# Gate and up projections by a seven-product block form on pairs of segments, in a fused attention and bilinear GLU kernel

## The chip, the cores and the metric

The kernel runs on one NeuronCore of a Trainium2 chip. A core has a matrix engine (TensorE, PE in the profile, with its weight loads as PEld), a vector engine (VectorE, DVE), a scalar engine (ScalarE, ACT), a general engine (GpSimd, POOL) and an engine that here only issues DMAs (SyncE, SP). Each engine takes its instructions in the order written in its own queue, and engines wait for one another through semaphores. The metric is the device time in microseconds (us).

## The reference, cut to what matters

There are 2048 tokens of width 512. An adaptive layer norm, an attention with a compressive memory over four segments of 512 tokens, and an output projection come first. Then a second layer norm and a bilinear gated unit with inner width F = 1376:

```python
x = x + ga * _A_ref(h, ...)                       # attention with output projection
h = _layernorm(x, axis=-1) * (1 + cb) + sb
g = jnp.einsum("bsd,df->bsf", h, w_gate)
u = jnp.einsum("bsd,df->bsf", h, w_up)
x = x + gb * jnp.einsum("bsf,fd->bsd", g * u, w_down)
```

Only the part from the second layer norm on is changed, with what is prepared for it at the end of the attention.

## The kernel before, in words

All matrix products of this part run in a fast 32-bit format (`float32r`), and to keep the precision each operand is split into a high part (a rounded copy) and a low part (the rest). One product is then three matmuls: high by high, low by high, high by low.

The attention part is written as one hand-ordered stream for PE (the helper `pe`, whose instructions all appear under L85 and L88). A loop over slots issues the attention's steps, and two generators, `fill_a` and `fill_b`, fill the gaps with projections. At the end, `fill_b` runs the output projection of segments 1 and 2 (`wo_mm`, `wo_row`, `wo_add`), the second layer norm of segment 0 (`lnC`), and the weights of the first two tiles of the inner width (`prep(0)`, `prep(1)`, on POOL). After the loop come the output projection of segment 3, in two steps: `wo_row` over the first three head groups, then the transpose and the rows of the last group. Each finished row of x is added by DVE and stored to DRAM (`x1d`) by SP.

Then the gated unit follows, segment by segment (called the last stage below). The inner width is cut into 11 tiles, ten of 128 and one of 96. `gate_up(i)` makes two PSUM banks of 12 matmuls each (four blocks of the 512-wide contraction by three splits, L1122); ACT copies the gate bank to SBUF (L1126), DVE multiplies it with the up bank (L1127), ACT rounds the product to its high part (L1130), DVE subtracts to get the low part (L1131). The down projection of tile i (L1143) comes after `gate_up(i + 1)` on PE and accumulates over all 11 tiles in four PSUM banks per segment; at the end of a segment DVE adds the four banks to x (L1156) and SP stores them (L1157). In segment 0 the weights of each next tile are loaded, split by DVE, ACT and POOL (L429 to L438) and kept for the later segments. The layer norm of the next segment is done inside the current one (at i = 3 and i = 6).

The program's order on each engine is made by a layer that places the instructions by its own costs; within one engine the order is then fixed.

Of the kernel before, what the change touches and what calls it, by code (L numbers as in the profile page):

```python
# [8 lines left out]
F32 = mybir.dt.float32  # L9
# [8 lines left out]
P = 128  # L18
S, D, H, DH, NSEG, L, F = 2048, 512, 32, 16, 4, 512, 1376
KT = D // P  # L20
NG = 4
# [36 lines left out]
def tile_kernel(ctx, tc, x, wq, wk_, wv, wo, beta, w_gate, w_up, w_down, c, w_mod, out):  # L58
# [34 lines left out]
    wpool = ctx.enter_context(tc.tile_pool(name="wp", bufs=1))  # L93
# [298 lines left out]
    wt = {}  # L392

    def prep(i, pool, rpool, tag, nb):

        f0, n = ft[i]
        r, raws = {}, {}
        for w, nm in ((w_gate, "g"), (w_up, "u")):
            raws[nm] = raw = rpool.tile([P, KT, P], F32, tag=tag, name=f"cr{nm}{i}", bufs=nb)
            pin(nc.sync.dma_start(raw[:, :, 0:n], w.rearrange("(k p) f -> p k f", p=P)[:, :, f0:f0 + n]))  # L400
        rawd = rpool.tile([P, D], F32, tag=tag, name=f"crd{i}", bufs=nb)
        pin(nc.sync.dma_start(rawd[0:n], w_down[f0:f0 + n, :]))
        yield 0.0
        if i < 2:
            gp = nc.gpsimd
            for nm in "gu":
                hi = pool.tile([P, KT, P], F32R, name=f"{nm}H{i}", bufs=1)
                r[nm] = (hi, pool.tile([P, KT, P], F32R, name=f"{nm}L{i}", bufs=1))
                pin(gp.tensor_copy(hi, raws[nm]))
                yield 0.0  # L410
            for nm in "gu":
                pin(gp.tensor_sub(r[nm][1], raws[nm], r[nm][0].bitcast(F32)))
                yield 0.0
            hi = pool.tile([P, D], F32R, name=f"dH{i}", bufs=1)
            lo = pool.tile([P, D], F32R, name=f"dL{i}", bufs=1)
            pin(gp.tensor_mul(rawd, rawd, gbb))
            yield 0.0
            pin(gp.tensor_copy(hi, rawd))
            yield 0.0
            pin(gp.tensor_sub(lo, rawd, hi.bitcast(F32)))  # L420
            r["d"] = (hi, lo)
            wt[i] = r
            yield 0.0
            return
        for nm in "gu":
            raw = raws[nm]
            hi = pool.tile([P, KT, P], F32R, name=f"{nm}H{i}", bufs=1)
            lo = pool.tile([P, KT, P], F32R, name=f"{nm}L{i}", bufs=1)
            pin(vec.tensor_copy(hi[:, :, 0:n], raw[:, :, 0:n]))  # L429
            nc.gpsimd.tensor_sub(lo[:, :, 0:n], raw[:, :, 0:n], hi[:, :, 0:n].bitcast(F32))  # L430
            r[nm] = (hi, lo)
            yield 0.0
        hi = pool.tile([P, D], F32R, name=f"dH{i}", bufs=1)
        lo = pool.tile([P, D], F32R, name=f"dL{i}", bufs=1)
        pin(vec.tensor_mul(rawd[0:n], rawd[0:n], gbb[0:n]))
        yield 0.0
        act.activation(hi[0:n], rawd[0:n], AF.Copy)
        nc.gpsimd.tensor_sub(lo[0:n], rawd[0:n], hi[0:n].bitcast(F32))  # L438
        r["d"] = (hi, lo)
        wt[i] = r  # L440
        yield 0.0
# [62 lines left out]
    def lnC(s, pool, hpool, xpool, tag, nb):  # L504
        xt = []
        for t in range(4):
            a = xpool.tile([P, D], F32, tag=tag, name=f"x1_{s}_{t}", bufs=nb)
            nc.sync.dma_start(a, x1d[s][t])
            xt.append(a)
        yield 0.1  # L510
        return (yield from ln(pool, hpool, xt, s, cb_c, sb_c, "c", ("h{}", 1, 1), s > 0))
# [429 lines left out]
    def fill_b():  # L941
# [7 lines left out]
        lg = lnC(0, pb, bc, pb, "x1", 4)  # L949
        pr = prep(0, bc, pb, "cr", 3)  # L950
# [135 lines left out]
    for t in range(4):  # L1086
        run(wo_row(ps3[t], t, us3, range(NG - 1)))
# [16 lines left out]
    for s in range(NSEG):  # L1104
# [30 lines left out]
        for i in range(NF):  # L1135
            if i + 1 < NF:
                gate_up(i + 1)
# [48 lines left out]
```

## Time and profile before

| | |
|---|---|
| median of 3 runs | 898.58 us (898.47 to 899.52) |
| profiled execution, its span from first to last instruction | 898.4 us; the page gives no other time of its own for it |
| PE busy | 870.9 us, 97% of the span |
| DVE, ACT, POOL busy | 523.4, 406.1, 321.2 us |
| last stage: first L1122 matmul to the start of the last L1143 matmul | 522.04 us to 893.50 us |
| mean granted TensorE clock | 0.993 |

A row of a timeline gives the start and the length of an instruction in us, the engine, the source line, the operation and its tiles, a count where rows are merged, and in brackets how long the engine had been idle and for whom it waited. A group row gives count, busy time in us and the mean of one instruction in ns, then the idle time ahead of the group. PE's matmuls are pipelined: the length of one in the profile is longer than the distance from one to the next, and it is the distance that counts. A row of stretches gives, for a stretch of time, each engine's busy time with its count, the granted clock, the busy share of the DMA engines and the rate in GB/s.

### The profile page before, as it was taken

How to read it: one execution, taken by the hardware profiler on the slowest of the kernel's cores; microseconds unless marked ns; L12 is line 12 of the kernel's file. 1: busy time of each engine (PE TensorE's matmuls, PEld its weight loads, DVE VectorE, ACT ScalarE, POOL GpSimd, SP SyncE). 2: the span in 40 equal slices, each digit the busy share in tenths (PEclk: the TensorE clock that was granted, in tenths of full speed). 3: DMA queues.
4: the chain of work that ended last, by engine and by line, in shares of the span. 5: the costliest groups of instructions: out<-in, count | busy, mean ns of one | idle time of the engine just before them, and what ended most of it. 6: DMA issues, size and time to landing. Idle time of an engine off the chain costs nothing.

```text
span 898.4 us, 14218 instructions
## 1 busy us (share of the span) xinstructions
PE 870.9 (97%) x5084; PEld 620.5 (69%) x5084; DVE 523.4 (58%) x1579; ACT 406.1 (45%) x601; POOL 321.2 (36%) x470
## 2 busy tenths in 40 slices
PE   8989999989999999999999999999999999999997
PEld 5755656556665556666666678887888788878886
DVE  7698777888788877778887244552133213321112
ACT  3747757687676865777454512231112111211111
POOL 4445536466455763756337516630000000000000
PEclk8999999999999999999999999999999999999999
DMA  7654434454545555365584344321001100110011
GB/s 219 163 159 130 122 109 124 152 154 130 146 111 156 141 154 129 107 202 166 187 243 140 109 144 126 106 73 71 24 1 47 72 24 1 47 45 3 1 47 47
DMA packets 74951, 97.23 MB, mean 108 GB/s; under 512 B 10528, under 2 KB 47392, under 8 KB 74880
## 3 DMA queue, kind: packets, MB, share of 16 engines
q1 hardware_dynamic: 74736, 96.31, 36.3%
q8 instruction: 40, 0.66, 0.3%
q14 instruction: 31, 0.25, 0.1%
q10 hardware_dynamic: 144, 0.02, 0.0%
HBM read 67.98 MB, written 28.05 MB: 107 GB/s over the span
## 4 chain that ended last, share of the span: by engine, by line
PE 81%; DVE 10%; ACT 5%; issue 1%; DMA 1%; POOL 1%; SPq 0%; DVEq 0%; POOLq 0%
PE gps L1122 14%; PE acc L1143 14%; PE ups L1122 14%; PE tb L85 8%; PE q L85 6%; PE k L85 6%; DVE q L39 5%; PE wops L85 5%; PE vps L85 4%; PE kps L85 4%; PE qps L85 2%; ACT pt L331 2%; PE up L85 1%; PE mz L85 1%; PE tr L88 1%
## 5 line engine op out<-in xcount | busy, mean ns | idle before, releaser
L39 DVE CUSTOM_DVE_ANT_0 q<-q,cmask 128x384 f32<-128x384 f32 (+3 forms) x512 | 246.6, 508 | 49.3 <-PE q L85 39.2
L331 ACT ACTIVATE pt<-k 128x1024 f32<-128x1024 f32 x160 | 163.8, 1024 | 64.4 <-PE k L85 63.3
L337 POOL TENSOR_SCALAR_AFFINE_SELECT pt<-pt 128x256 f32<-128x256 f32 (+1 forms) x224 | 96.7, 446 | 166.0 <-ACT pt L331 163.6
L1127 DVE TENSOR_TENSOR gs<-gs,ups 128x512 f32<-128x512 f32 (+1 forms) x44 | 30.2, 687 | 194.9 <-PE ups L1122 194.9
L85 PE MATMUL q<-kst,qst 96*128 96x384 bf16 (+3 forms) x512 | 101.6, 299 | 11.0 <-DVE nm L39 9.7
L85 PE MATMUL k<-qst,kst 98*128 98x384 bf16 (+3 forms) x512 | 97.1, 302 | 5.0 <-ACT pt L331 4.9
L1126 ACT ACTIVATE gs<-gps 128x512 f32<-128x512 f32 (+1 forms) x44 | 26.2, 597 | 146.3 <-PE gps L1122 146.3
L1130 ACT ACTIVATE mH<-gs 128x512 fp32r<-128x512 f32 (+1 forms) x44 | 27.8, 632 | 130.4 <-DVE gs L1127 128.1
L85 PE MATMUL tb<-pt,v 128*32 128x512 f32 (+3 forms) x1024 | 75.5, 436 | 0.0
L39 DVE DVE_READ_ACCUMULATOR2_ANT nm<- 128x1 f32 x512 | 72.2, 141 | 0.0
L85 PEld LDWEIGHTS <-kst 98*128 98x128 bf16 x512 | 37.7, 98 | 49.5 <-issue 43.2
L1122 PE MATMUL gps<-chH,gL 128*128 128x512 f32 (+1 forms) x176 | 69.3, 394 | 0.0
L1122 PE MATMUL gps<-chH,gH 128*128 128x512 f32 (+1 forms) x176 | 69.3, 394 | 0.0
L1143 PE MATMUL acc<-dH,mL 128*128 128x512 f32 (+1 forms) x176 | 69.3, 394 | 0.0
L1122 PE MATMUL ups<-chH,uH 128*128 128x512 f32 (+1 forms) x176 | 69.3, 394 | 0.0
L1122 PE MATMUL gps<-chL,gH 128*128 128x512 f32 (+1 forms) x176 | 69.3, 393 | 0.0
L1143 PE MATMUL acc<-dL,mH 128*128 128x512 f32 (+1 forms) x176 | 69.2, 393 | 0.0
L1122 PE MATMUL ups<-chL,uH 128*128 128x512 f32 (+1 forms) x176 | 69.2, 393 | 0.0
L1122 PE MATMUL ups<-chH,uL 128*128 128x512 f32 (+1 forms) x176 | 69.2, 393 | 0.0
L85 PEld LDWEIGHTS <-qst 96*128 96x128 bf16 x512 | 43.1, 97 | 37.5 <-issue 13.4
L1143 PE MATMUL acc<-dH,mH 128*128 128x512 f32 (+1 forms) x176 | 65.0, 395 | 0.0
L85 PEld LDWEIGHTS tb<-pt,v 128*32 128x32 f32 x1024 | 28.7, 109 | 38.6 <-issue 33.8
(218 smaller groups left out, 1654.5 us busy)
## 6 DMA issues: line engine op xcount, KB each, us to landing
wm<-in_w_mod_dram SPq DMA_DIRECT2D x24, 256.0 KB, 4.0
kd<-k SPq DMA_DIRECT2D x16, 384.0 KB, 2.5
kst<-kd SPq DMA_DIRECT2D x32, 192.0 KB, 3.2
qd<-q SPq DMA_DIRECT2D x16, 384.0 KB, 2.9
qst<-qd SPq DMA_DIRECT2D x32, 192.0 KB, 3.6
x<-in_x_dram SPq DMA_DIRECT2D x16, 256.0 KB, 4.5
kst<-kd SPq DMA_DIRECT2D x32, 128.0 KB, 3.1
qst<-qd SPq DMA_DIRECT2D x32, 128.0 KB, 3.6
```

The source lines that it names most:

```text
L39: i = getattr(self.eng, name)(*a, **k)
L85: return pe(nc.tensor.matmul(*a, **k))
L88: return pe(nc.tensor.transpose(*a))
L331: ex = act.activation(pt, kp, AF.Exp, scale=0.25)
L337: sels[u, i] = nc.gpsimd.affine_select(w, w, pattern=[[0, w.shape[1]], [1, P]], compare_op=ALU.is_ge, fill=0.0, base=0, channel_multiplier=-1)
L1122: nc.tensor.matmul(ps[0:n], a[:, k, 0:n], b[k], start=j == 0, stop=j == 11)
L1126: act.activation(gs[0:n], pss[0][0:n], AF.Copy)
L1127: vec.tensor_mul(gs[0:n], gs[0:n], pss[1][0:n])
L1130: act.activation(mH[0:n], gs[0:n], AF.Copy)
L1143: nc.tensor.matmul(acc[t], a[0:n, t * P:(t + 1) * P], b[0:n, :], start=i == 0 and j == 0, stop=i == NF - 1 and j == 2)
```

## The change

The last stage works on pairs of segments (0 and 1, then 2 and 3) and pairs of inner tiles. The 512-wide contraction is cut in two halves, the pair of segments gives the other cut of the moving operand, and the pair of tiles that of the weights: a product of 2 by 2 blocks. Instead of eight block products, seven are computed (Winograd's variant of Strassen's form). A block product is six matmuls (two blocks of 128 of the contraction by three splits). One `unit` makes one pair of tiles of gate or of up for both segments: 42 matmuls, in the order of products 2, 5, 1, 3, 6, and the last two, 7 and 4, are issued inside the following unit. Results and partial sums stay in three kinds of PSUM banks (Z, Y, X); products 6, 7 and 4 are accumulated onto X after the sum so far has been read by DVE or ACT. The odd tile of 96 has no partner and is done by `last_unit` with the plain four block products per segment.

- The moving blocks: `build` makes, once per pair of segments, seven pieces (the four blocks are kept as full 32-bit tiles `hf`; POOL makes the four differences t1 to t4, ACT and DVE split every piece in high and low).
- The weights: `wprep` loads the weights of a unit (one DMA of 512 KB), makes four sums and differences on POOL (S), and splits seven blocks, with ACT for the high and POOL for the low parts. This is done for each pair of segments, so every weight is loaded and prepared twice; there are three sets of weight tiles, and the preparation of unit n + 2 goes with unit n. `wdprep` does the same for the down weights.
- The parts of a unit's result are put together by DVE (c0, c1, c2). For an up unit, gate by up is multiplied by POOL for three of the four blocks and by DVE for the fourth.
- Down: the product of two tiles (six matmuls) goes to a PSUM bank and DVE adds it to x in SBUF, for each of 4 row tiles of 2 segments and each pair of tiles. The row tiles of a group of down products are queued and given out one at a time inside the following units.
- At the end of the attention: the layer norm of segment 1 is moved in front of the last stage, into the output projection of segment 3; the weights prepared there are those of unit 0 alone, and those of unit 1 follow when the attention's memory is free.

```diff
+    def wprep(n, tag, pool, rpool):
...
+        pin(nc.sync.dma_start(raw.rearrange("p k r c -> p k (r c)"), views["gu".index(nm)][:, :, 0:2 * P]))
+        yield
...
+        gp.tensor_add(S[:, 0], A(1, 0), A(1, 1))
+        gp.tensor_sub(S[:, 1], S[:, 0], A(0, 0))
+        yield
+        gp.tensor_sub(S[:, 2], A(0, 0), A(1, 0))
+        gp.tensor_sub(S[:, 3], A(0, 1), S[:, 1])
+        yield
+        top = raw[:, :, 0].rearrange("p (c k) f -> p c k f", c=2)
+        for d, v in ((slice(4, 6), top), (6, A(1, 1)), (slice(0, 4), S)):
+            act.activation(wh[:, d], v, AF.Copy)
+            gp.tensor_sub(wl[:, d], v, wh[:, d].bitcast(F32))
+            yield
...
-    for t in range(4):
-        run(wo_row(ps3[t], t, us3, range(NG - 1)))
...
+    lg = lnC(1, pb, B["bc"], pb, "x1", 7, lqbank)
+    rows3 = (w for t in range(4) for w in wo_row(ps3[t], t, us3, range(NG - 1)))
+    run(weave(rows3, lg, (0, 0, 0, 0, 0, 0, 2, 3, 4, 5, 7, 8, 9, 10)))
...
-        def gate_up(i):
...
+    def build(p):
+
+        def emit(j, srcs):
...
+            for k in range(2):
+                act.activation(hi[:, k], srcs[k], AF.Copy)
+                vec.tensor_sub(lo[:, k], srcs[k], hi[:, k].bitcast(F32))
+            pieces[p, j] = hi, lo
...
+        emit(2, b21)
+        yield
+        t1 = comb("t1", b12, b11)
+        emit(5, t1)
+        yield
+        emit(1, b11)
+        yield
+        emit(3, b22)
+        yield
+        t2 = comb("t2", b22, t1)
+        emit(6, t2)
+        yield
+        emit(7, comb("t3", b22, b12))
+        yield
+        emit(4, comb("t4", b21, t2))
+        yield
...
+    def six(ps, wh, wl, wi, n, bh, bl, first, last):
+        c = 0
+        for k in range(2):
+            w, l = (a[(slice(None), *wi(k), slice(0, n))] for a in (wh, wl))
+            for a, b in ((w, bh), (l, bh), (w, bl)):
+                pe(nc.tensor.matmul(ps[0:n], a, b[:, k], start=first and c == 0, stop=last and c == 5, skip_group_check=True))
+                c += 1
...
+    def split(p, f, c, h):
...
+        act.activation(mH[0:n], h[0:n], AF.Copy)
+        vec.tensor_sub(mL[0:n], h[0:n], mH[0:n].bitcast(F32))
...
+    def wdprep(p, f):
...
+        pin(nc.sync.dma_start(r[0:n], w_down[f0:f0 + n, :]))
+        yield
+        vec.tensor_mul(r[0:n], r[0:n], gbb[0:n])
+        act.activation(hi[0:n], r[0:n], AF.Copy)
+        vec.tensor_sub(lo[0:n], r[0:n], hi[0:n].bitcast(F32))
...
+    def down(p, fs, c, t):
+        ps = dbank(f"acc{p}_{fs[0]}_{c}_{t}")
...
+            for a, b in ((mH, dH), (mL, dH), (mH, dL)):
+                pe(nc.tensor.matmul(ps, a[0:m, t * P:(t + 1) * P], b[0:m], start=j == 0, stop=j == n - 1))
+                j += 1
+        xa = x1a[p, c, t]
+        vec.tensor_add(xa, xa, ps)
...
+    def finish(p, nm, f, c, v, psum):
...
+        g = gs.pop((p, f, c))
+        (vec if psum else nc.gpsimd).tensor_mul(g[0:n], g[0:n], v[0:n])
+        split(p, f, c, g)
...
+    def unit(n):
...
+        Z = pst((P, 512), "sm", f"Z{u}")
+        mm(Z, 2, True, True)
+        yield 1
+        prev(0)
+        Y = pst((P, 512), "tb", f"Y{u}")
+        mm(Y, 5, True, True)
+        p5 = out_of(f"p5{u}", Y)
+        yield 2
+        X = xbank(f"X{u}")
+        mm(X, 1, True, True)
+        finish(p, nm, i, 0, add(f"c0{u}", Z, out_of(f"p1{u}", X)), False)
+        yield 3
+        prev(1)
+        tail.clear()
+        yield 4
+        mm(Y, 3, False, True)
+        yy = out_of(f"y{u}", Y)
+        yield 5
+        mm(X, 6, False, True)
+        finish(p, nm, i, 1, add(f"c1{u}", X, yy), False)
+        yield 6
+
+        def seven():
+            mm(X, 7, False, True)
+            finish(p, nm, i + 1, 1, add(f"c2{u}", X, p5), False)
+
+        def four():
+            mm(X, 4, False, True)
+            finish(p, nm, i + 1, 0, X, True)
+            if nm == "u":
+                dq.extend(lambda c=c, t=t: down(p, (i, i + 1), c, t) for c in (1, 0) for t in range(4))
+
+        tail.extend((seven, four))
...
+    pr1 = prepare(1)
+    for _ in range(6):
+        next(pr1)
+    run(build(0))
+    DS = {"g": (1, 5, 6), "u": (1, 2, 4, 5, 6), "x": (1, 4, 6)}
...
+    for n in range(2 * NU):
+        nm, i = units[n % NU]
+        pr = prepare(n + 2)
...
+        for st in (unit if nm != "x" else last_unit)(n):
+            next(pr, None)
...
+            if st in DS[nm] and n < 2 * NU - 1:
+                d()
...
+            if (n - NU + 1, st) in ((0, 1), (0, 2), (0, 3), (0, 5), (0, 6), (1, 2), (1, 4)):
+                next(nb)
```

In the changed program the engines' queues stand as follows at the start of the last stage. SP: the four stores of x of segment 3, then the weights of unit 1, those of unit 2, two down weights, eight tiles of x. ACT: the high parts of pieces 2, 1, 3 and 5, then those of unit 1's first weight block, of piece 6 (first half), of unit 2's first weight block, of piece 6 (second half), and then the copies of products 5 and 1 of unit 0. DVE: the four adds of x of segment 3, then the low parts of pieces 2, 1, 3, 5 and 6. POOL: t1 and t2, two sums of unit 1's weights, t3 and half of t4, two sums of unit 2, the first low part of unit 1, the rest of t4, and then the remaining sums and low parts of units 1 and 2 in turn, the widest (128x1024) last.

More of the change, by code (lines that the diff above doesn't have):

```diff
@@ new lines, in prepare @@
+    def prepare(n):
+        if n >= 2 * NU:
+            return
+        yield from wprep(n, n % 3, bc if n % 3 == 0 else pc, bc if n % 2 == 0 else pc)
+        nm, i = units[n % NU]
+        if nm == "u":
+            yield from wdprep(n // NU, i)
+            yield from wdprep(n // NU, i + 1)
+        elif nm == "x":
+            yield from wdprep(n // NU, LAST)
+    half = [(c, t) for c in (1, 0) for t in range(4)]
+    for c, t in half:
+        xtile(0, c, t)
+    pr1 = prepare(1)
+    for _ in range(6):
+        next(pr1)
@@ L1158, in tile_kernel @@
+    tail[0]()
+    d()
+    tail[1]()
+    d(99)
     close(pcpool)
```

315 lines of the change are left out of this document (202 added, 113 removed).

## The prediction

> **What bounds the kernel now.** I read the busy shares first, then stretches of the last stage, then its groups and its two ends in the timeline.
>
> ```profile
> PE 870.9 (97%) x5084; PEld 620.5 (69%) x5084; DVE 523.4 (58%) x1579; ACT 406.1 (45%) x601; POOL 321.2 (36%) x470
> PE 81%; DVE 10%; ACT 5%; issue 1%; DMA 1%; POOL 1%; SPq 0%; DVEq 0%; POOLq 0%
> ```
>
> ```profile
> core 0: us, PE busy (x) PEld busy (x) DVE busy (x) ACT busy (x) POOL busy (x), PEclk, DMA share, GB/s
> 509.00:522.00 13.00, 11.99 (x52) 9.54 (x53) 3.73 (x8) 0.60 (x1) 1.47 (x2) 1.00 0.08 29
> 522.00:600.00 78.00, 78.00 (x346) 63.39 (x345) 40.59 (x66) 19.72 (x33) 37.23 (x31) 1.00 0.42 124
> 600.00:700.00 100.00, 100.00 (x444) 80.88 (x443) 28.66 (x49) 18.16 (x30) 3.17 (x7) 1.00 0.10 35
> ...
> 20.00:24.00 4.00, 4.00 (x14) 3.32 (x13) 2.76 (x6) 3.50 (x5) 0.00 (x0) 0.50 0.44 131
> 24.00:28.00 4.00, 4.00 (x17) 3.24 (x16) 2.48 (x5) 2.16 (x5) 0.00 (x0) 0.86 0.01 2
> 895.90:896.90 1.00, 0.00 (x0) 0.00 (x0) 0.00 (x0) 0.00 (x0) 0.00 (x0) 0.50 0.95 367
> ```
>
> ```profile
> 522.04 0.39 PE L1122 MATMUL gps<-chH,gH 128*128 128x512 f32 x1
> ...
> 893.50 0.39 PE L1143 MATMUL acc<-dL,mH 96*128 96x512 f32 x1
> 893.92 0.69 DVE L1156 TENSOR_TENSOR xc<-xc,acc 128x512 f32<-128x512 f32 x1 [0.34 <-PE acc L1143]
> ```
>
> ```profile
> 500.63 0.60 PE L88 MATMUL ctp<-ident,x 128*128 128x128 f32 x4
> 500.98 0.48 PE L85 MATMUL wops<-woH,oH 128*128 128x512 f32 x1
> ```
>
> The last stage is PE alone: no gap from 522 on, while ACT and DVE are busy less than a third of 600 to 700 and POOL is nearly free. It lasts 371.46 us (522.04 to 893.50) and holds 4 segments x 11 tiles x (24 + 12) = 1584 matmuls and 48 small transposes. Four transposes take 0.35 us of PE (500.63 to 500.98), 48 take 4.2, so a matmul costs 367.3 / 1584 = 0.232 us. POOL's 37 us before 600 are the weights, made once. The span, 898.4 us, stands 0.2 below the median of 898.58, which I take as the base; 0.2% of it, about 1.8 us, is what a measurement of this kernel can tell from no change.
>
> **Matmuls removed.** Per pair of segments there are now ten units of 42 and one of 48 matmuls, 936 in two pairs instead of 4 x 11 x 24 = 1056. Down keeps its 528. So 120 x 0.232 = 27.8 us leave PE. The 16 transposes of segment 1 (1.4 us) move ahead of the stage and cost the same there. At the end one add follows the last matmul, not two: -0.6.
>
> **Work added beside PE.** Per gate and up unit together PE has 84 + 48 = 132 matmuls, 30.6 us.
>
> ```profile
> L1126 ACT ACTIVATE gs<-gps 128x512 f32<-128x512 f32 x40 | 23.8, 597 | 128.8 <-PE gps L1122 128.8
> L1130 ACT ACTIVATE mH<-gs 128x512 fp32r<-128x512 f32 x40 | 25.3, 632 | 118.9 <-DVE gs L1127 116.6 <-issue 2.3
> L331 ACT ACTIVATE pt<-k 128x1024 f32<-128x1024 f32 x160 | 163.8, 1024 | 64.4 <-PE k L85 63.3 <-POOL pt L337 0.4
> L571 POOL TENSOR_TENSOR hmg<-hmg,gg 128x128 f32<-128x128 f32 x4 | 1.5, 402 | 0.0
> ```
>
> ```profile
> 472.87 1.27 POOL L412 TENSOR_TENSOR uL<-cru,uH 128x512 fp32r<-128x512 f32 x1
> 473.24 0.69 DVE L39 TENSOR_TENSOR oL<-op,oH 128x512 fp32r<-128x512 f32 x1
> ...
> 534.33 1.35 POOL L430 TENSOR_TENSOR gL<-crg,gH 128x512 fp32r<-128x512 f32 x1 [22.70 <-DVE gH L429]
> 534.55 1.67 DVE L1131 TENSOR_TENSOR mL<-gs,mH 128x512 fp32r<-128x512 f32 x1
> 535.63 1.74 POOL L430 TENSOR_TENSOR uL<-cru,uH 128x512 fp32r<-128x512 f32 x1
> 536.15 1.77 DVE L435 TENSOR_TENSOR crd<-crd,gbb 128x512 f32<-128x512 f32 x1
> ```
>
> ACT: 7 copies at 0.60, 6 roundings at 0.63, weights 2 x (0.63 + 0.35 + 1.02) = 12 us. DVE: 6 sums, 1 product and 8 adds of down that read PSUM, and 8 operations from SBUF alone, 23 x 0.69 = 16 us. POOL: from 0.40 at 128 wide and 1.27 at 512 I estimate 0.69 at 256 and 2.4 at 1024; a unit's weights are four sums and three low parts, 4 x 0.69 + 1.27 + 0.69 + 2.4 = 7.1, two units and three products 18. All fit into 30.6 in sum. What need not fit is the moment. The last four rows show that a DVE operation with both inputs in SBUF and a POOL operation exclude each other: mL took 1.67 instead of 0.69, uL 1.74 instead of 1.27, each ending about 0.55 or 1.15 after the other let go. The two rows above them show that a DVE operation reading PSUM does not wait.
>
> Where PE needs DVE soonest is c1: after product 6 comes the next unit's product 2, at most with one down between, 12 matmuls or 2.8 us, and then product 7 on the same bank. If DVE stands behind a 2.4 us operation of POOL with one low part ahead of c1, that is 2.4 + 0.6 + 0.7 + 0.3 of hand-overs = 4.0, 1.2 us uncovered. With 40 hand-overs (c1 and c2 in 20 units) the bounds are 0 and 48. I take one in six, 8 us, including the second `build`, whose 14 roundings, 14 low parts and 8 differences fall among these.
>
> **The layer norm of segment 1, moved.**
>
> ```profile
> 506.99 0.33 SPq L496 DMA_DIRECT2D x1d<-xr  x1
> 509.01 0.33 SPq L480 DMA_DIRECT2D xr<-in_x_dram  x1
> 509.09 0.50 PE L85 MATMUL wops<-woH,oH 128*128 128x512 f32 x1 [0.34 <-DVE oL L39]
> ...
> 480.29 0.18 DVE L39 BATCH_NORM_AGGREGATE cmv<-cst 128x2 f32<-128x6 f32 x1
> 481.96 0.20 POOL L195 TENSOR_TENSOR cy<-cy,cyb 128x4 f32<-128x4 f32 x1
> 484.52 0.53 DVE L39 TENSOR_SCALAR x<-x,cmv,cy 128x512 f32<-128x512 f32 x1
> ```
>
> ```profile
> x<-x1d SPq DMA_DIRECT2D x16, 256.0 KB, 2.8
> crg<-in_w_gate_dram SPq DMA_DIRECT2D x10, 256.0 KB, 3.4
> ```
>
> Three of its four loads stand on SP behind the load at 509.01, which waits for a buffer: issued until 510.2, the last lands at 513.0. Statistics of that tile about 0.9, then 1.7 from the aggregate's end (480.47) to the scale (482.16), then four scalings of 0.53: 516.1 to 517.7. PE comes to the first transposes after 8 rows of 3 matmuls, at 509.1 + 5.5 = 514.6, and leaves them at 517.9 instead of 514.95. That is 2.9; with loads 2 us later 5, with earlier loads 0. The weights of unit 0 put 7 us of POOL and 2 of ACT into the attention, where two tiles' weights left; bounds -1 and +2, I take 0.6. Together 3.5.
>
> **The start of the stage.** T is the first product.
>
> ```profile
> 520.17 2.76 DVE L39 TENSOR_TENSOR xr<-xr,wops 128x512 f32<-128x512 f32 x4 [0.82 <-PE wops L85]
> 520.89 2.39 SPq L496 DMA_DIRECT2D x1d<-xr  x4
> 523.37 0.40 SPq L400 DMA_DIRECT2D crg<-in_w_gate_dram  x1
> ```
>
> DVE is in the four adds of x until T + 0.9, SP in their stores until T + 1.3 (523.37 against 522.04), as before; before, nothing on PE waited for either.
> - Product 2 needs its low piece at T + 0.5 and gets it at 1.6: 1.1.
> - Product 5: its low piece is the seventh on DVE, T + 0.9 + 7 x 0.62 = 5.2, PE is there at 3.0: 2.2. Product 1 ends at 8.0.
> - Product 3 reuses the bank of product 5, whose copy stands on ACT behind the first weight blocks of units 1 and 2. Loads of 256 KB land in 3.4; for 512 KB I take 4.5, and 2 more for the second: 5.8 and 7.9. Then 0.98 and 0.63 and 0.6: 10.1, 2.1 lost.
> - Unit 1's first low part is ninth on POOL from the first load on: two sums, t3, t3, half of t4, two sums, itself: 4 x 0.69 + 4 x 1.27 = 7.8, with four DVE turns of 0.55 in between T + 15.8. PE is there at 13.2: 2.6.
> - Product 7 needs c1 behind seven SBUF operations of DVE, each sharing with POOL: 2.5.
> - Product 5 of unit 1 needs the 128x1024 low part: seven POOL operations, 6, and itself 2.4, with DVE's turns 2.8: T + 27.5 against 21.2: 6.3.
> - The first down products wait for a chain of POOL, ACT and DVE: 3.5.
>
> Sum 20.3. Without any sharing, and with the loads on time, the first two and half of the sixth stay, 7; with slower loads, a POOL a fifth slower and the later waits of the next units, 32.
>
> ```profile
> 523.83 1.72 SPq L400 DMA_DIRECT2D cru<-in_w_up_dram  x1
> ```
>
> This row shows the second of two such loads held for 1.7 us on SP itself, which speaks against an earlier landing.
>
> **The clock.** The stretches above show the granted clock at 0.50 in 20 to 24, with PE busy, after its loose work in 12 to 20, and at 0.50 again 2.4 us after the last matmul (895.9). So a pause of PE of a few us is followed by matmuls at half speed. One such return cost 4 us at half speed, 2 us; I take one: 2. The Trainium skill ("TensorE: Matmul & The Clock Gate", Part 1) says that one idle window of about 3.4 us halves the clock and a busy one restores it; by that an estimate of 1.7 us per pause would come out, and only the pause of 6.3 would count. The trace's fall to 0.50 by 895.9 comes only 2 us after the last matmul ended at 893.9, sooner than the page's window; so the row decides here.
>
> **Sum.** -27.8 - 0.6 + 3.5 + 20.3 + 8 + 2 = +5.4: 904.0 us.
>
> **Rivals.**
> - *The start is mostly covered and the sharing seldom bites*, on the other side: start 9, hand-overs 2, no half clock, norm 3: 898.6 - 28.4 + 14 = 884. It decides as soon as all waits together stay under 28.4 us. For it speaks that ACT, DVE and POOL have 18, 14 and 12 us free of 30 in each pair of units; against it the two rows of exclusion and the in-order casts behind a load. 878 to 896.
> - *The clock stays at half through the start.* Four pauses over 2 us follow each other within 30 us; if the clock returns only after the last one, some 20 us of matmuls at half speed cost 10 more, and with 3 to 5 more in the queues that then lag: 904 + 14 = 918. The row at 20 to 24 speaks for it, and that PE is still busy over half of that time against it.
> - *It does what it was cut down to and no more*: all added work hidden, 898.6 - 28.4 + 3 = 873.
>
> **How the numbers follow.** The forecast, slower by some units of us (900.5 to 912, own range): 0.45. Within 0.2%, which is the same sum with two or three terms at their smaller ends: 0.09. The covered start: 0.31, of which all hidden 0.03. The half clock: 0.15. Faster 0.31, same 0.09, slower 0.60. The range 881 to 918 leaves out about 2 in 10: all hidden and the lower part of the covered start, and the upper half of the half clock.
>
> **What the profile will show.** If right: 120 matmuls fewer in the stage; idle PE ahead of product 3 of unit 0 with the copy p5 as releaser, and ahead of unit 1's first and fifth products with POOL's low parts as releasers; most of PE's idle time in the first 50 us; low parts of DVE with a mean well over 0.7 us and POOL's differences over 1.3; the first transposes of segment 1 waiting for DVE for about 3 us; hand-over waits on c1 and c2, 1 to 2 us each. The prediction is wrong if the stage has no PE gap over 2 us at its start (the loads came in time or other work came first), if low parts and POOL operations run side by side at their own lengths, if a clock of 0.5 lasts tens of us, or if the distance between matmuls, 0.232, is another with this mix of loads.

## The result, and the profile after

The changed kernel takes 910.23 us (median of 4 runs, 909.49 to 910.30) against 899.0 us for the kernel before (4 runs, 898.47 to 899.52): 1.0122 times as long, 95% interval 1.0108 to 1.0137. It is slower by 11.2 us, twice the 5.4 us of the forecast, and inside the range of 900.5 to 912 that the forecast gave itself.

The busy shares and the engines' shares of the chain of the changed kernel, lines from its page:

```profile
PE 853.1 (94%) x4963; PEld 598.7 (66%) x4964; DVE 652.7 (72%) x1712; ACT 479.8 (53%) x732; POOL 502.7 (55%) x615
PE 68%; DVE 15%; ACT 7%; POOL 3%; DMA 3%; issue 3%; SPq 0%; DVEq 0%; ACTq 0%; POOLq 0%
```

PE has 121 matmul records fewer, where 120 are due, and is busy 17.8 us less, but the chain that ended last runs over DVE, ACT and POOL for 25% of the span instead of 16%. Five marks in PE's timelines show where the time went. First the kernel before, then the one after; the marks are the transposes of the last head group (`tr`), and after it the first product, the first product of units 2 and 3, and the last matmul.

```profile
508.09 0.66 PE L88 MATMUL tr<-ident,tsb 128*128 128x128 f32 x4 [0.42 <-DVE oL L39]
```

```profile
508.93 0.66 PE L88 MATMUL tr<-ident,tsb 128*128 128x128 f32 x4 [0.41 <-DVE oL L39]
...
530.40 0.39 PE L1186 MATMUL Zg<-bH,cwH 128*128 128x512 f32 x1
...
566.10 0.39 PE L1186 MATMUL Zg<-bH,cwH 128*128 128x512 f32 x1
...
582.77 0.39 PE L1186 MATMUL Zu<-bH,cwH 128*128 128x512 f32 x1
...
904.46 0.39 PE L1242 MATMUL acc<-dL,mH 128*128 128x512 f32 x1
```

With the rows of before that the prediction shows (522.04 and 893.50), the two profiled executions compare like this:

| stretch | before, us | after, us | difference | forecast |
|---|---|---|---|---|
| start to `tr` | 508.09 | 508.93 | +0.84 | +0.6 |
| `tr` to the first product | 13.95 | 21.47 | +7.52 | +4.3 (2.9, and 1.4 for 16 transposes moved) |
| first product to last matmul | 371.46 | 374.06 | +2.60 | +1.1 (-27.8 - 1.4 + 20.3 + 8 + 2) |
| last matmul to the end | 4.9 | 4.04 | -0.86 | -0.6 |
| span | 898.4 | 908.5 | +10.1 | +5.4 |

The last 1.1 us are outside this table: the listed runs of either kernel last about 1.7 us longer than their spans. By that the profiled execution of before, 898.4 in span, would be one of 900.1 us, 1.1 above the median; its own time is not on record.

### The profile page after: what moved, and what is told of

It is laid out like the page before. It is cut to its first block, busy times and chain, and to the rows that moved or that the text cites. A ratio compares the mean times of both kernels' runs of the same rounds, so it can differ in the third digit from the quotient of the medians.

```text
span 908.5 us, 14393 instructions
## 1 busy us (share of the span) xinstructions
PE 853.1 (94%) x4963; PEld 598.7 (66%) x4964; DVE 652.7 (72%) x1712; ACT 479.8 (53%) x732; POOL 502.7 (55%) x615
## 4 chain that ended last, share of the span: by engine, by line
PE 68%; DVE 15%; ACT 7%; POOL 3%; DMA 3%; issue 3%; SPq 0%; DVEq 0%; ACTq 0%; POOLq 0%
PE acc L1242 11%; PE tb L85 7%; PE q L85 6%; PE k L85 6%; PE Xg L1186 5%; PE Xu L1186 5%; PE vps L85 5%; DVE q L39 4%; PE wops L85 4%; PE kps L85 3%; PE Yu L1186 3%; PE qps L85 3%; PE Yg L1186 2%; ACT pt L331 2%; PE Zu L1186 1%
## 5 line engine op out<-in xcount | busy, mean ns | idle before, releaser
L1245 DVE TENSOR_TENSOR xa<-xa,acc 128x512 f32<-128x512 f32 x95 | 64.8, 682 | 47.4 <-PE acc L1242 45.7
L1242 PE MATMUL acc<-dH,mH 128*128 128x512 f32 (+1 forms) x174 | 68.5, 394 | 0.0
L435 POOL TENSOR_TENSOR cwL<-cs,cwH 128x1024 fp32r<-128x1024 f32 x20 | 52.4, 2624 | 4.0 <-ACT cwH L434 4.0
L435 POOL TENSOR_TENSOR cwL<-cr,cwH 128x512 fp32r<-128x512 f32 (+1 forms) x40 | 43.7, 1112 | 12.7 <-ACT cwH L434 12.7
L1270 POOL TENSOR_TENSOR c0g<-c0g,c0u 128x512 f32<-128x512 f32 x10 | 12.9, 1293 | 60.7 <-DVE c0u L1275 46.6
L1186 PE MATMUL Xu<-bH,cwH 128*128 128x512 f32 (+1 forms) x88 | 36.1, 410 | 6.2 <-DVE c2u L1275 4.0
L363 ACT ACTIVATE tsb<-tb 128x512 f32<-128x512 f32 x32 | 19.0, 594 | 40.2 <-PE tb L85 40.2
L1242 PEld LDWEIGHTS acc<-dH,mL 128*128 128x128 f32 (+1 forms) x174 | 32.8, 189 | 9.3 <-DVE mL L1211 2.3
L1242 PEld LDWEIGHTS acc<-dH,mH 128*128 128x128 f32 (+1 forms) x174 | 32.8, 189 | 8.2 <-ACT mH L1210 0.4
L1242 PEld LDWEIGHTS acc<-dL,mH 128*128 128x128 f32 (+1 forms) x174 | 32.7, 188 | 7.1
```

The costliest lines, as they stand in the source:

```text
L363: act.activation(tsbs[u], tbs.pop(u), AF.Copy)
L435: gp.tensor_sub(wl[:, d], v, wh[:, d].bitcast(F32))
L1186: pe(nc.tensor.matmul(ps[0:n], a, b[:, k], start=first and c == 0, stop=last and c == 5, skip_group_check=True))
L1242: pe(nc.tensor.matmul(ps, a[0:m, t * P:(t + 1) * P], b[0:m], start=j == 0, stop=j == n - 1))
L1245: vec.tensor_add(xa, xa, ps)
L1270: (vec if psum else nc.gpsimd).tensor_mul(g[0:n], g[0:n], v[0:n])
```

## Where the last stage loses time

PE's rows of the start in which it had waited, up to the first product of unit 2 and a little on, changed kernel; the bracket gives the wait and its releaser:

```profile
531.94 0.50 PE L1186 MATMUL Zg<-bL,cwH 128*128 128x512 f32 x1 [0.91 <-DVE bL L1150]
...
535.55 0.50 PE L1186 MATMUL Yg<-bL,cwH 128*128 128x512 f32 x1 [1.94 <-DVE bL L1150]
...
540.45 0.69 PE L1186 MATMUL Yg<-bH,cwH 128*128 128x512 f32 x1 [2.31 <-ACT p5g L1295]
...
546.59 0.50 PE L1186 MATMUL Zu<-bH,cwL 128*128 128x512 f32 x1 [1.29 <-POOL cwL L435]
...
555.39 0.80 PE L1186 MATMUL Yu<-bH,cwH 128*128 128x512 f32 x1 [5.96 <-ACT cwH L434]
...
557.81 0.80 PE L1186 MATMUL Yu<-bH,cwL 128*128 128x512 f32 x1 [1.62 <-POOL cwL L435]
...
568.01 0.50 PE L1186 MATMUL Xu<-bH,cwH 128*128 128x512 f32 x1 [0.39 <-DVE c1u L1275]
```

Stretches of the same kernel (busy time of each engine with its count, then the clock):

```profile
530.40:582.80 52.40, 36.66 (x128) 26.48 (x127) 31.59 (x38) 21.65 (x38) 45.77 (x36) 0.87 0.46 152
582.80:680.00 97.20, 97.00 (x438) 77.64 (x437) 62.77 (x91) 37.94 (x65) 54.18 (x54) 1.00 0.20 59
680.00:760.00 80.00, 74.64 (x318) 58.90 (x318) 64.28 (x75) 36.19 (x63) 67.99 (x52) 1.00 0.28 87
760.00:905.00 145.00, 143.00 (x618) 113.93 (x616) 82.53 (x112) 41.03 (x70) 60.15 (x50) 1.00 0.16 48
```

Up to unit 3 PE has 126 matmuls of 0.232 us, 29.2 us, and takes 52.4: 23.1 lost. The seven waits are 14.4 of them, and two more, of 1.07 and 0.23 us, stand inside the first down product, at 576.65 and 577.85; the other 7.4 are matmuls at half clock (0.87 in the stretch) and restarts. From there on 1338 matmuls and 32 transposes are due in 313.2 us and take 321.7: 8.5 lost, 5.4 of it as idle time of PE at 680 to 760, where the pieces of the second pair are made and POOL is busy for 68 of 80 us. PE's waits behind 582.77 are seven for c1 and c2, 7.2 us in sum, and one of 0.2. So the stage lost 31.6 us; the forecast had 30.3.

## The experiments

All kernels compute the same result as the changed kernel. Single runs of one kernel spread over 0.8 to 6.5 us here, so a difference of a median under 2 us is not read as one; inside a trace, distances between the marks are used. The changed kernel itself was measured once, ahead of the experiments; the kernel before, measured again with each group of them, had medians of 898.55 to 899.73, so a gain against 910.23 is uncertain by about 1 us from this alone. A trace is of one execution: those of the run with 13 extra matmuls (907.98), of unit 1's early load (906.80) and of the start alone (899.86) are of the fastest of their runs.

**PE kept busy ahead of the norm's transposes.**

```diff
             ps = bk(f"ctp{s}_{d}")
+            if s == 1 and d == 2:
+                for _ in range(13):
+                    MM(ps, B["us3"][0][0][:, 0:P], B["wo"][0][0], start=True, stop=True)
```

> Edit: 13 matmuls whose result is overwritten (the output does not change) are put on PE ahead of the first transposes of segment 1, where PE stood idle for 3.22 us; nothing else. Theory A, the pause halves the clock: in the changed kernel three groups of transposes and seven matmuls took 5.62 us from 518.53 to 524.15, where 3 x 0.35 + 7 x 0.232 = 2.7 are due; without the pause they take 2.7 and the time falls by about 2.9, to 907.3. Theory B, these rows are slow because the two banks of the transposes wait for ACT: no gain, 910.2.

Measured 909.93 us (907.98 to 912.85), 1.0132 times before (1.0111 to 1.0153).

```profile
507.56 0.66 PE L88 MATMUL tr<-ident,tsb 128*128 128x128 f32 x4 [0.41 <-DVE oL L39]
...
517.32 1.70 PE L88 MATMUL ctp<-ident,x 128*128 128x128 f32 x4 [0.44 <-DVE x L39]
...
527.59 0.40 PE L1189 MATMUL Zg<-bH,cwH 128*128 128x512 f32 x1
```

From `tr` to the first product it takes 20.03 us instead of 21.47: the half clock behind the norm's pause cost 1.4, half of what theory A had. The first four transposes still take 1.70 us, so these are not slow by the clock: each waits for its own scaling on DVE. The lead of 1.4 still stands at the first matmul of unit 1's product 5 (45.1 us behind `tr` instead of 46.5) and is gone at unit 2 (57.1 and 57.2), mainly because half clock behind that wait lasted 14 matmuls here and 7 there. The time is theory B's number, though not for its reason; A is right on the place and wrong on what it is worth.

**PE kept busy in more waits of the start.**

```diff
+        if n == 1:
+            warm(4)
         Z = pst((P, 512), "sm", f"Z{u}")
...
+        if n < 2:
+            warm((7, 22)[n])
         Y = pst((P, 512), "tb", f"Y{u}")
...
+        if n == 0:
+            warm(8)
         mm(Y, 3, False, True)
```

> Edit: as the run with 13 extra matmuls before the norm's transposes, and 3, 7, 8, 4 and 22 extra ones into an unused bank where PE waited at the start of the last stage (before product 5 and product 3 of unit 0, before unit 1, before its product 5; the 3 fit none of the waits exactly). Theory A, half clock costs on top of the waits: of the 23 us that the stage loses up to 582.8, 15 are idle and some 1.6 are restarts, so about 6.5 are half clock; with the 2.9 of the norm the time falls by 9.4, to 900.8. Theory B, the half clock before unit 1's product 5 is hidden, since that product waits for POOL and ACT whatever PE does before: only 3 of the 6.5 come back, 904.3. Theory C, no clock at work: 910.2 or slower.

The edit has groups of 7, 8, 4 and 22 beside the 13 of the run before; the group of 3 that the expectation names is not in it. Measured 910.89 us (909.62 to 911.28), ratio 1.0129 (1.0114 to 1.0145): the time of theory C. `tr` to unit 2 is 54.7 us instead of 57.2, so what the extra matmuls took away was worth 2.4 us up to there, far from theory A's figure. It was not all of the half clock: PE still waited 1.20, 1.22 and 0.72 us around unit 1's first product, nine matmuls from 546.09 to 551.02 went at 0.43 us instead of 0.23, and the granted clock of the first two units is 0.90, where the changed kernel has 0.86. Of the 2.4 us, 1.7 are lost again behind unit 2, part of them in a longer wait for the first down products (1.75 us instead of 1.07): `tr` to the last matmul is 394.8 us instead of 395.5, and the time shows nothing of the 0.8 left.

**The norm's whole head earlier.**

```diff
+                lg = lnC(1, B["pb"], B["bc"], B["pb"], "x1", 8, lqbank)
+                next(lg)
                 o3 = wo_load(3, wpool)
...
+                for _ in range(9):
+                    next(lg)
```

> Edit: loads, statistics and scaling of the norm of segment 1 are issued ahead of the loads and the transposes of segment 3's projection instead of inside its rows, with one more buffer for x; same work. Theory A, the move of the norm cost 3.22 us of waiting and 2.9 of half clock: both go, 904.1. Theory B, the norm's DVE steps then delay the splits that the rows of the projection wait for, or the loads delay x of segment 3: the wait reappears a few us earlier, 908 to 911.

Measured 913.71 us (913.17 to 914.08), ratio 1.0163 (1.0148 to 1.0178).

```profile
515.79 1.12 PE L88 MATMUL tr<-ident,tsb 128*128 128x128 f32 x4 [4.88 <-DVE oL L39]
```

Theory B, and more than it said: the four scalings, waiting for the statistics, stood on DVE ahead of the splits of segment 3, and PE waited 4.88 us for those. From `tr` to the first product it is then 17.06 us: the norm's own wait is gone.

**Unit 1's load and sums early.**

```diff
-        raw = rpool.tile([P, KT, 2, P], F32, tag=f"raw{n % 2}", name=f"cr{n}", bufs=1)
+        raw = rpool.tile([P, KT, 2, P], F32, tag=f"raw{n and (n + 1) % 2}", name=f"cr{n}", bufs=1)
...
                 xr3 = xr_load(3, B["pb"])
+                pr1 = wprep(1, 1, False, B["bc"])
+                next(pr1)
...
+    next(pr1)
+    next(pr1)
```

> Edit: the raw weights and the four sums of unit 1 use the buffers that unit 0 has left, so its load and its sums are issued during the rows of segment 3's projection; ACT's and POOL's splits of unit 1 stay in the last stage; same work. Theory A, the start is lost to the late load and the chain of POOL behind it: the waits of 2.31 (behind ACT's cast), 1.29, 5.96 and 1.62 us go, and half clock behind the long one, 11 to 14 us: 896 to 899. Theory B, POOL's low parts and the sharing with DVE are the limit and the load is not: unit 1 still waits for the 128x1024 low part, gain under 5 us, 905 or more.

Measured 908.95 us (906.80 to 911.17), ratio 1.0111 (1.0087 to 1.0134). The four waits of theory A went, and PE waited for DVE instead, 2.73 and 5.64 us, inside products 2 and 5 of unit 0:

```profile
532.08 10.35 DVE L1161 TENSOR_TENSOR bL<-chf,bH 128x512 fp32r<-128x512 f32 x6
```

Six low pieces took 1.7 us each, since POOL was now busy beside them from the first product on. The first two units came down from 35.7 to 30.6 us. Theory B holds in its cause (sharing), though not at the place it named.

**The order of the pieces bound.**

```diff
-                vec.tensor_sub(lo[:, k], srcs[k], hi[:, k].bitcast(F32))
+                (vec if p else CV).tensor_sub(lo[:, k], srcs[k], hi[:, k].bitcast(F32))
...
+    for _ in range(3):
+        next(pr1)
+        next(bd)
```

> Edit: as the run with unit 1's load and sums early, and the low pieces of the first pair are bound on DVE to the order in which PE uses them (2, 5, 1, 3, 6, 7, 4), ACT's casts of unit 1 stand among the pieces instead of ahead of them, those of unit 2 behind the copy p5. All operations stay on their engines. In the run before, DVE's six low pieces took 10.35 us, 1.7 each, while POOL worked, and PE waited 2.73 and 5.64 us for two of them. Theory A, sharing: with POOL's differences and low parts still beside them the pieces stay at 1.2 to 1.7 us each, PE still waits 4 us or more for them, time 904 to 909. Theory B, it was only the order: the two waits fall under 2 us in sum, time under 903.

Measured 908.51 us (907.72 to 910.90), ratio 1.0113 (1.0096 to 1.0129). Theory A: PE waits for the pieces six times, 6.6 us in sum (2.04, 0.41, 0.28, 1.80, 0.72, 1.31), and 2.45 us for c0 of unit 0 at the start of unit 1; four pieces take 6.82 us, 1.7 each.

**POOL out of the start.**

```diff
+        gl = CV if n == 1 else nc.gpsimd
...
-            gp.tensor_sub(wl[:, d], v, wh[:, d].bitcast(F32))
...
+            gl.tensor_sub(wl[:, d], v, wh[:, d].bitcast(F32))
...
-                nc.gpsimd.tensor_sub(t, a[k], b[k])
+                (CV if (p, nm) in ((0, 't3'), (0, 't4')) else nc.gpsimd).tensor_sub(t, a[k], b[k])
```

> Edit: as the run with the order bound (e5_order), and the differences t3 and t4 and the low parts of unit 1's weights, 7 of POOL's operations, are done by DVE, so that POOL has nothing to do between the first product and the sums of unit 2; the same results. DVE gets 7 operations more, about 5.2 us of work. Theory A, sharing sets the start: the low pieces take 0.7 us each, the first two units (30.6 us in the run with unit 1 early, 35.7 in the changed kernel) come down to 22 to 25, and the time is 4 to 8 us under that of e5_order, 898 to 902. Theory B, DVE's load itself is the limit: with 5 us more on DVE it is 0 to 5 us slower than e5_order.

Measured 912.86 us (909.24 to 913.05), ratio 1.0147 (1.0127 to 1.0167). DVE and then POOL of this kernel:

```profile
534.30 1.29 DVE L39 TENSOR_TENSOR bL<-chf,bH 128x512 fp32r<-128x512 f32 x2
535.52 1.29 DVE L39 TENSOR_TENSOR bL<-t,bH 128x512 fp32r<-128x512 f32 x2
536.74 1.29 DVE L39 TENSOR_TENSOR bL<-chf,bH 128x512 fp32r<-128x512 f32 x2
```

```profile
540.07 4.22 POOL L433 TENSOR_TENSOR cs<-cr 128x256 f32<-128x256 f32 x1 [6.98 <-DMA cr<-in_w_gate_dram]
```

The lengths are as theory A has them: 0.64 us a piece instead of 1.7, and the first sum of unit 2, which took 0.73 us alone, took 4.22 while DVE ran one operation after the other. The time is not, it is theory B's number, 4.4 us over the run before: PE now waited 5.86 us for the copy p5, which stood on ACT behind piece 7 and so behind t3 on DVE, and 6.29 us for c1, which stood on DVE behind the down weights. The first two units took 35.4 us. So sharing was not the only cause. Whether the orders on DVE and ACT or the 5 us more of work on DVE took its place, this run does not separate; the run with the orders written out below bears on it.

**Loads and statistics of the norm early, the scaling where it was.**

```diff
+            if v == NQ - 1 and slot == 0:
+                lg = lnC(1, B["pb"], B["bc"], B["pb"], "x1", 8, lqbank)
+                next(lg)
...
+                for _ in range(5):
+                    next(lg)
...
-    run(weave(rows3, lg, (0, 0, 0, 0, 0, 0, 2, 3, 4, 5, 7, 8, 9, 10)))
+    run(weave(rows3, lg, (0, 0, 0, 0, 7, 8, 9, 10)))
```

> Edit: only the loads and the statistics of the norm of segment 1 are issued earlier (the loads one slot of the attention ahead, the statistics behind the last loads of segment 2's projection); the scaling stays where it was, behind the splits that held PE for 4.88 us when it was put ahead of them. Theory A: the transposes find their data (PE is there at about 515.3, the scaling can be done by 513), the wait of 3.22 us goes with the half clock behind it (1.6 by the run with 13 extra matmuls): 4.8 less from the transposes of the last head group to the first product, about 16.7 instead of 21.5 us, and 905.5. Theory B: the loads or the statistics hold up segment 2's or 3's x and PE waits there: no gain.

Measured 905.12 us (904.35 to 906.95), ratio 1.0073 (1.0058 to 1.0088): theory A, 5.1 us under the changed kernel.

```profile
508.92 0.66 PE L88 MATMUL tr<-ident,tsb 128*128 128x128 f32 x4 [0.41 <-DVE oL L39]
515.10 0.60 PE L88 MATMUL ctp<-ident,x 128*128 128x128 f32 x4
...
524.27 0.39 PE L1189 MATMUL Zg<-bH,cwH 128*128 128x512 f32 x1
```

`tr` to the first product is 15.35 us, 1.40 more than in the kernel before, which are the 16 transposes. So the move of the norm had cost 21.47 - 15.35 = 6.1 us beyond them.

**POOL out of the rest of the stage.**

```diff
-        gp = nc.gpsimd
+        gp = vec if n > 2 else nc.gpsimd
+        gl = vec if n > 2 else nc.gpsimd
...
-            gp.tensor_sub(wl[:, d], v, wh[:, d].bitcast(F32))
+            gl.tensor_sub(wl[:, d], v, wh[:, d].bitcast(F32))
...
-                nc.gpsimd.tensor_sub(t, a[k], b[k])
+                (vec if p == 1 else nc.gpsimd).tensor_sub(t, a[k], b[k])
...
-        (vec if psum else nc.gpsimd).tensor_mul(g[0:n], g[0:n], v[0:n])
+        (vec if psum or (p, f) not in ((0, 0), (0, 1)) else nc.gpsimd).tensor_mul(g[0:n], g[0:n], v[0:n])
```

> Edit: from unit 3 on, everything that POOL did (sums, differences and low parts of the weights, three products of gate and up, the four differences of the second pair) is done by DVE; the start is unchanged. POOL has about 180 us of work there, which is about 100 us on DVE by 0.69 against 1.27 us; DVE would be busy for some 320 of 330 us if its operations kept their present lengths, and for some 260 if those that now share fall to 0.7. Theory A, the 8 to 9 us that PE loses behind unit 2 come from sharing: the waits for c1 and c2 go, 902 to 904. Theory B, they come from DVE's queue being long: they grow, 912 to 925.

Measured 904.36 us (904.10 to 908.46), ratio 1.0076 (1.0050 to 1.0101): on theory A's side, 0.4 over its range and 5.9 us under the changed kernel. Unit 2 to the last matmul takes 331.5 us instead of 338.4. Of these 6.9 us, 2.6 lie in unit 2, where the waits of the first down product are gone, and 4.3 behind it; the waits for c1 and c2 behind unit 2 did not go but fell from 7.2 to 4.3 us. Groups of the two kernels from 585 to 890 us (busy us, mean ns). First the changed kernel:

```profile
L435 POOL TENSOR_TENSOR cwL<-cs,cwH 128x1024 fp32r<-128x1024 f32 x15 | 40.2, 2677 | 3.0 <-ACT cwH L434 3.0
L1211 DVE TENSOR_TENSOR mL<-c0g,mH 128x512 fp32r<-128x512 f32 x9 | 12.7, 1415 | 6.6 <-ACT mH L1210 6.6
L1150 DVE TENSOR_TENSOR bL<-t,bH 128x512 fp32r<-128x512 f32 x8 | 11.0, 1369 | 0.3 <-ACT bH L1149 0.2
```

Then this experiment:

```profile
L436 DVE TENSOR_TENSOR cwL<-cs,cwH 128x1024 fp32r<-128x1024 f32 x15 | 18.3, 1221 | 2.0 <-ACT cwH L435 1.8
L1212 DVE TENSOR_TENSOR mL<-c0g,mH 128x512 fp32r<-128x512 f32 x9 | 6.1, 683 | 0.7 <-ACT mH L1211 0.7
```

The low part of a weight block takes DVE less than half of what it took POOL, and the low parts of the products fall, in the group shown from 1.4 to 0.68 us, over the four blocks of 128 rows from 1.04 to 0.69. The same stretch as a whole, the changed kernel and then this one:

```profile
585.00:890.00 305.00, 297.60 (x1298) 236.72 (x1297) 200.57 (x262) 115.16 (x197) 180.20 (x151) 1.00 0.20 58
```

```profile
585.00:890.00 305.00, 299.98 (x1317) 240.97 (x1316) 237.57 (x407) 114.79 (x197) 4.93 (x10) 1.00 0.20 58
```

DVE took over 175 us of POOL's time and is busy only 37 us more, since its own operations are shorter. How much of PE's gain comes from the end of the sharing, and how much from operations that are shorter on DVE than on POOL, the run does not separate.

**The norm and the rest of the stage together** (both diffs in one kernel).

> Edit: the earlier loads and statistics of the norm (905.1) and POOL's work from unit 3 on given to DVE (904.4) in one kernel. If the two are terms of one sum, 5.1 and 5.9 us add up: 899.2, level with the kernel before. If one hides the other (the queues behind the norm and those of the stage are one chain), 902 to 905.

Measured 897.88 us (median of 10 runs, 896.2 to 902.67), ratio 0.9994 (0.9979 to 1.0008): the two add up, and with both edits the kernel is level with the one before.

**The start alone, with its orders written out.**

```diff
+        gp = vec if n == 2 else nc.gpsimd
+        gl = vec if 1 <= n <= 2 else nc.gpsimd
...
+    vec.eng, act.eng = CV, CA
...
+        if n == 0:
+            early[3] = prepare(3)
+            plan = {1: [pr], 2: [wd[0], wd[1]], 3: [bd], 6: [w1, bd]}
+        elif n == 1:
+            plan = {1: [p2, p2], 2: [p2, pr], 3: [p2, wd[0]], 4: [p2, wd[1]], 5: [pr], 6: [pr]}
+        else:
+            plan = None
+            vec.eng, act.eng = nc.vector, nc.scalar
```

(`CV` and `CA` keep the order of writing on DVE and ACT; `plan` says behind which step of a unit the next step of a piece, a weight block or a down weight is written.)

> Edit: the start alone. Unit 1's load and sums early; POOL makes the differences t1, t2, t3 before the first product, DVE makes t4, the low parts of units 1 and 2 and the sums of unit 2; DVE and ACT keep in units 0 and 1 the order in which PE needs the results (the sums so far c0 and c1 ahead of pieces 7 and 4, the copies p5, p1 and y ahead of what waits for a load or a difference). From unit 3 on nothing is changed. In the run without sharing the low pieces took 0.64 us each and PE then waited 5.86 us for p5 behind ACT's piece 7 and 6.29 us for c1 behind the down weights. Theory A, the start loses 23 us to sharing and to orders on DVE and ACT, no bandwidth being short: the first two units take 22 to 26 us instead of 35.7, and the time is 898 to 902. Theory B, DVE has more to do in the start than PE's products cover, whatever the order: 30 us or more, 905 or slower.

Measured 902.94 us (median of 8 runs, 899.86 to 905.48), ratio 1.0046 (1.0031 to 1.0060): 7.3 us gained, a time between the two theories' ranges, 0.9 above A's and 2.1 below B's. In the trace the first two units took 24.6 us, within theory A's 22 to 26, with more of POOL's work on DVE than in the run with POOL out of the start (35.4): DVE's load is not what held that one. The orders were changed together with the place of unit 2's weights, so the parts of the two are not separated; unit 2 of the new run then took 18.8 instead of 16.7, with a wait of 3.18 us for c1 of unit 1.

**All three.**

> Edit: the start as in e10_start, the norm's earlier loads and statistics, and all of POOL's work from unit 2 on given to DVE. If the three terms add up (5.1, 5.9 and about 10 us) the time is 888 to 892, faster than the kernel before by 0.7 to 1.2%. If they are one chain of DVE that only changes its place, 897 to 904.

Measured 890.75 us (890.38 to 891.19), ratio 0.9910 (0.9894 to 0.9927): faster than both kernels, and 19.5 us under the changed one, where the three gains alone sum to 18.3 (taken by the ratios to the kernel before, about 19.1 against 4.4 + 4.1 + 6.8 = 15.3). PE's first product, the longest wait that is left, and the last matmul:

```profile
524.43 0.39 PE L1201 MATMUL Zg<-bH,cwH 128*128 128x512 f32 x1
...
553.10 0.79 PE L1201 MATMUL Xu<-bH,cwH 128*128 128x512 f32 x1 [5.57 <-DVE c1u L39]
...
884.62 0.39 PE L1257 MATMUL acc<-dL,mH 128*128 128x512 f32 x1
```

**That wait taken away.**

```diff
-            plan = {1: [p2, p2], 2: [p2, pr], 3: [p2, wd[0]], 4: [p2, wd[1]], 5: [pr], 6: [pr]}
+            plan = {1: [p2, p2], 2: [p2, pr], 3: [p2], 4: [p2], 6: [wd[0], wd[1]]}
+        elif n == 2:
+            plan = {1: [pr], 3: [p3], 4: [p3, p3], 5: [p3], 6: [p3]}
```

> Edit: as e11_all, and DVE and ACT keep the order of need through unit 2 as well: c1 of unit 1 ahead of the first down weights and of the weights of units 3 and 4. In e11_all PE waited 5.57 us for that c1 and ran at half clock behind it (0.84 in the 20 us). Theory A, c1 stood behind work that nobody needed yet (2.6 us of down weights, about 2.3 of sums): 4 us of the wait and most of the half clock go, 884.5 to 887.5. Theory B, DVE is full in the first 30 us, and what is put back is missed by the first down products or by unit 3: 889 to 893.

Measured 891.70 us (889.26 to 893.75), ratio 0.9910 (0.9884 to 0.9935): theory B. The wait for c1 fell to 0.33 us, and these came:

```profile
556.70 0.50 PE L1201 MATMUL Xu<-bH,cwH 128*128 128x512 f32 x1 [2.33 <-DVE c2u L39]
...
596.19 0.50 PE L1257 MATMUL acc<-dH,mL 128*128 128x512 f32 x1 [2.27 <-DVE mL L1226]
```

First product to last matmul is 359.9 us here and 360.2 in the run before: DVE is busy for 26.0 of the first 30 us here and 27.0 there, and an order chooses who waits. Some 18 us over the 342.4 that PE needs remain: by the matmuls due (0.232 us each) 5.3 lie in the first two units, 4.6 in the third and 7.6 behind it. What would take them away was not tried.

## Why the forecast was half of the loss

- **Matmuls removed (-27.8) and the end (-0.6): right.** 1464 matmuls at 0.232 us explain the stretches without waits; the end gave 0.86.
- **The layer norm of segment 1 (2.9): this step failed.** It cost 6.1 us beyond its transposes, by the run with early loads and statistics, and 5.1 of the time. The mechanism was right, PE waiting behind a late load and DVE; the size was too small, in the lateness of the loads and in the clock. DVE's rows of the changed kernel, the statistics of the third and fourth tile and the scaling, then PE's, the first transposes and the row behind them:

```profile
514.50 0.69 DVE L39 BATCH_NORM_STATS2 cst<-x 128x6 f32<-128x512 f32 x1 [0.54 <-DMA x<-x1d]
...
515.33 0.66 DVE L39 BATCH_NORM_STATS2 cst<-x 128x6 f32<-128x512 f32 x1
...
517.93 1.92 DVE L39 TENSOR_SCALAR x<-x,cmv,cy 128x512 f32<-128x512 f32 x4 [1.72 <-POOL cy L526]
```

```profile
518.53 1.70 PE L88 MATMUL ctp<-ident,x 128*128 128x128 f32 x4 [3.22 <-DVE x L39]
519.98 0.66 PE L85 MATMUL wops<-woH,oH 128*128 128x512 f32 x1
```

  The third of four loads ended at 514.5, where the prediction had the last one at 513.0, and the statistics of two tiles, not of one, stood behind it. The last scaling ended at 519.85 instead of 517.7. PE, ready at about 515.15, left the first transposes at 519.98, after 3.22 us of waiting and then at the pace of the scalings: 4.5 us late, where the prediction had 2.9 for the same. The second part is the clock: it stayed at half for the next rows, 1.4 by the run with 13 extra matmuls, and the prediction had given its one half clock to the start. 4.5 + 1.4 is 5.9 of the 6.1. The prediction had 5 as its bound for loads 2 us later, and took 2.9.
- **The start (20.3, and 2 for the clock): right in sum, not in its terms.** 23.1 against 22.3; that the sums agree is luck. The waits for the low pieces (0.91, 1.94 against 1.1, 2.2), for p5 (2.31 against 2.1) and for unit 1's product 5 (5.96 and 1.62 against 6.3) came near the sizes worked out (the parts of the last one add up to T + 27.0 and 5.8). The releasers were those named, but for the 5.96: it ended on ACT's high part of the weights, and only the 1.62 behind it on POOL's low part. The wait for c1 of unit 0 (2.5) did not come, and c1 of unit 1 cost 0.39; of those for the first down products (3.5) 1.3 came, and unit 1's first product waited half of its 2.6. In their place stood half clock and restarts, 7.4 instead of 2. What taking a part of it away is worth, the runs with extra matmuls show: 2.4 us up to unit 2, with the norm's, and 0.8 at the last matmul.
- **Hand-overs (8): right in size.** 8.5 behind unit 2, with seven waits of the 40 hand-overs, as the one in six of the prediction. When POOL's work there went to DVE, 4.3 of the 8.5 came back. The prediction named the exclusion as their cause, from two rows; the group means of that run show that the exclusion lengthened DVE's operations, but not that all of the waits come from it.
- **The base.** The sum was made against a span of 898.4 as if that execution were a median one; by the table it was 1.1 us slower than the median. Between the forecast 904.0 and the measured 910.2 lie 6.2 us: 3.2 from the norm, 1.5 from the stage, 1.1 from the base, and 0.4 since the median of before is 899.0 now.
- **The rivals.** The covered start did not happen, and the runs show what it takes: with the norm's loads early, the orders of the start written out and POOL's work on DVE the kernel is at 890.75, within the range of 878 to 896 that the rival had. That the clock stays at half through the start is refuted by the changed kernel's own rows: behind the pause of 2.31 us eight matmuls went at 0.43 to 0.49 us, and from 544.21 on they are 0.23 apart again.

## What to carry to other kernels

Before an engine is given work because it is idle, look at whether it excludes another one: here DVE took over 175 us of POOL's time for 37 us more of its own, and the kernel got 5.9 us shorter. When a stage of a saturated engine gets shorter by some 7%, as here, its start and the hand-overs decide, so write the order of need on every helper queue, and issue loads by when they are needed rather than where the code that uses them stands. Price a moved step by its last load, with all that stands between that load and the engine that waits, and by the clock behind the pause.

## What the hardware showed that was not expected

- Between DVE and POOL there was no fair turn. In the start of the changed kernel they alternated, each operation waiting for one of the other's; but against a DVE that had its next operation ready, one POOL operation of 128x256 took 3.5 us longer than alone (4.22 instead of 0.73), while five operations of DVE ran at their own lengths. The Trainium skill ("SBUF — State Buffer", Who interferes with whom) says that the two engines share a port pair by an exclusive lock; the trace agrees with the exclusion (0.64 us a piece without POOL, 1.7 with it).
- Extra matmuls in PE's waits removed a part of the half clock (from `tr` to the first product the granted clock rose from 0.92 to 1.00, in the first two units from 0.86 to 0.90) and saved nothing that could be measured in the time.
- Which pause halves the clock is not a matter of its length alone. Behind a pause of 2.04 us in the run of the start alone the matmuls went at half clock, 0.43 us apart up to 534.39; behind 2.47 us in the run with POOL out of the rest of the stage they were 0.23 apart from the second on:

```profile
531.24 0.79 PE L1198 MATMUL Zg<-bL,cwH 128*128 128x512 f32 x1 [2.04 <-DVE bL L39]
531.83 0.63 PE L1198 MATMUL Zg<-bH,cwH 128*128 128x512 f32 x1
```

```profile
727.82 0.50 PE L1187 MATMUL Xg<-bH,cwH 128*128 128x512 f32 x1 [2.47 <-DVE c1g L1276]
728.15 0.40 PE L1187 MATMUL Xg<-bH,cwL 128*128 128x512 f32 x1
```

  Half clock need not begin with the first matmul behind a pause: in the last experiment, behind the 2.33 us at 556.70, the first two are at full speed, and the matmuls are 0.43 us apart from 557.56 to 560.55. The Trainium skill ("TensorE: Matmul & The Clock Gate", Part 1) gives an idle window of about 3.4 us that runs freely; pauses shorter than this halved the clock here, so the length of one pause alone does not decide it.
